# The second and third load on SyncE's queue, swapped, in a LayerNorm + S5 + SwiGLU kernel

## The chip, the cores and the metric

The kernel runs on one core of a Trainium2 chip. The metric is the device time of one execution in microseconds (us); lower is better. A profile is one execution seen by the hardware profiler, and its times count from the start of the span. TensorE (PE, with PEld for its weight loads), VectorE (DVE), ScalarE (ACT), GpSimd (POOL) and SyncE (SP) are the engines of the core. SyncE does no arithmetic here; it issues DMAs. ScalarE issues some as well, on a queue of its own.

## What is computed

The input x has 2048 rows of 512 in bfloat16. With xn the layer-normalised x, the result is the sum of x, a diagonal state-space model (S5) of xn and a SwiGLU block of xn:

```
xn  = layernorm(x)
Bu  = xn @ B_bar^T                 # complex, 512 states
h_t = Lam_bar * h_(t-1) + Bu_t     # over the 2048 rows
y   = 2 * real(h @ C^T) + xn * Dskip
ffn = (silu(xn @ w_gate) * (xn @ w_up)) @ w_down     # 1376 hidden columns
out = x + y + ffn
```

## The kernel before

The 2048 rows are 16 x tiles of 128 rows (`xall[:, n, :]`), and four tiles make a chunk of 512 rows. For a chunk, TensorE needs xnT, the transposed normalised rows, as its moving operand. The products with w_gate and w_up (`gu_mm`, L425; `w_last` L451 and L461), with B (`bproj_tile`, L350), with w_down (L505) and with C (L514) run over the chunks in an order that is written out by hand at the end of the kernel. VectorE's work (scan, rotations, tables, products) is put between them by a backlog with a cost for each operation, which `pump` works off.

w_gate and w_up are loaded in column groups (`fgroups`): group 0 holds the hidden columns of tiles 0 and 1, group 1 those of tiles 2 and 3, then 4 to 6 and 7 to 9. A group is one tile in SBUF, wg0 to wg3 for gate and wu0 to wu3 for up, and one DMA by `load_w1` (L110 to L112; all of them show as L112). Groups 0 and 1 have 256 KB each, in rows of 512 bytes. An x tile has 128 KB, in rows of 1024 bytes.

The loads are issued in program order on each engine (L123 to L154). Before the change SyncE issues x tile 0, wg0, x tile 2, wg1, wu1, x tiles 4 and 5, x tiles 6 and 7, wg2, wu2, the transposes of B's real part, wg3, wu3, and so on. ScalarE issues x tile 1 (held back behind a VectorE memset of a part of that tile, L124), wu0 and x tile 3. GpSimd loads three small parameter rows. Each DMA counts up one of eight completion semaphores, which the DMAs take in turn; a DMA that takes one for the second time is issued only when the earlier DMA on it has landed.

The first chunk is done tile by tile (the head, L600 to L650), because its tiles arrive one after the other:

- TensorE first runs nine warming matmuls that nobody reads (`dummy`, L574).
- For tile n, VectorE takes the row statistics (`ln_stats`, L178 and L179; L604 and L606 for tile 1, L619 and L621 for tile 3), ScalarE makes the inverse deviation (L183, L184), VectorE normalises (`norm_dve`, L196), TensorE transposes (`xT_pe`, L213), and VectorE (L220) or ScalarE (L222) copies the result from PSUM into xnT.
- Between these, `head_mm` (L597) multiplies the tiles that are there with the groups that are there: first tile 0 with wg0, then (after tile 1's transposes) tile 0 with wu0, tile 1 with both, then tiles 0 and 1 with hidden tile 2, which is the first use of wg1, then tile 2's transposes and the transpose of the parameter rows (L243), then wu1, and so on.

The engines wait only through semaphores, so a weight load that waits for its DMA holds up all TensorE instructions behind it.

Of the kernel before, what the change touches and what calls it, by code (L numbers as in the profile page):

```python
# [23 lines left out]
def kernel(  # L24
# [17 lines left out]
    nc = tc.nc  # L42
# [36 lines left out]
    x_v = A_x[0].rearrange("(n p) d -> p n d", p=128)  # L79
    out_v = out[0].rearrange("(n p) d -> p n d", p=128)  # L80
    wg_v = B_w_gate.rearrange("(k p) f -> p k f", p=128)
    wu_v = B_w_up.rearrange("(k p) f -> p k f", p=128)


    xall = const.tile([128, NT, D], BF16, name="xall")
# [3 lines left out]
    wg_g, wu_g = [], []  # L89
# [20 lines left out]
    def load_w1(q, tiles, view, gi):  # L110
        a, b = fgroups[gi]
        q.dma_start(out=tiles[gi][:], in_=view[:, :, a * 128:min(F, b * 128)])  # L112
# [10 lines left out]
    nc.sync.dma_start(out=xall[:, 0, :], in_=x_v[:, 0, :])  # L123
    nc.vector.memset(xall[:, 1, 0:D // 2], 0.0)  # L124
    nc.scalar.dma_start(out=xall[:, 1, :], in_=x_v[:, 1, :])
    load_w1(nc.sync, wg_g, wg_v, 0)
    load_w1(nc.scalar, wu_g, wu_v, 0)
    nc.sync.dma_start(out=xall[:, 2, :], in_=x_v[:, 2, :])
    nc.scalar.dma_start(out=xall[:, 3, :], in_=x_v[:, 3, :])
    load_w1(nc.sync, wg_g, wg_v, 1)  # L130
    load_w1(nc.sync, wu_g, wu_v, 1)
# [638 lines left out]
```

## Time and profile before

| what | value |
|---|---|
| time, median of 3 runs (lowest, highest) | 179.78 us (179.71, 179.78) |
| time of the profiled execution | 179.83 us |
| its span | 178.1 us |
| mean granted TensorE clock | 0.999 |
| TensorE, busy time | 173.7 us |
| VectorE, busy time | 153.3 us |
| DMA traffic over the whole span | 15.53 MB, mean 87 GB/s |
| SyncE's DMA queue (q1), ScalarE's (q10), share of 16 engines' time | 28.9%, 1.4% |

Busy time is the time in which an engine executes instructions; waits for semaphores are not in it. The chain of work that ended last is followed back from the last instruction, at each step to what released it. In the lists of instructions a line gives start and length in us, the engine (SPq and ACTq are DMA issues by SyncE and ScalarE), the line in the kernel, the operation, what it writes and reads, its shape and how many are merged; in brackets stands the idle time of the engine before it and what ended that idle time. "us to landing" of a DMA counts from the start of its issue to the last of its 16 completion counts.

### The profile page before, as it was taken

How to read it: one execution, taken by the hardware profiler on the slowest of the kernel's cores; microseconds unless marked ns; L12 is line 12 of the kernel's file. 1: busy time of each engine (PE TensorE's matmuls, PEld its weight loads, DVE VectorE, ACT ScalarE, POOL GpSimd, SP SyncE). 2: the span in 40 equal slices, each digit the busy share in tenths (PEclk: the TensorE clock that was granted, in tenths of full speed). 3: DMA queues.
4: the chain of work that ended last, by engine and by line, in shares of the span. 5: the costliest groups of instructions: out<-in, count | busy, mean ns of one | idle time of the engine just before them, and what ended most of it. 6: DMA issues, size and time to landing. Idle time of an engine off the chain costs nothing.

```text
span 178.1 us, 2462 instructions
## 1 busy us (share of the span) xinstructions
PE 173.7 (98%) x916; PEld 83.2 (47%) x916; DVE 153.3 (86%) x233; ACT 94.2 (53%) x173; POOL 23.2 (13%) x29
## 2 busy tenths in 40 slices
PE   7899999999999999999999999999999999999993
PEld 2784444444444444444444444444444444444743
DVE  3789997999999999999999999999999999940033
ACT  3579696978499966033997660024866610220000
POOL 6003000001400000029100000013405000150000
PEclk9999999999999999999999999999999999999999
DMA  5998956994236400021920000007286900073012
GB/s 159 327 254 204 144 98 174 361 184 104 44 76 218 180 0 0 0 29 14 137 61 0 0 0 0 4 0 81 29 125 84 156 2 0 0 79 39 4 48 70
DMA packets 29131, 15.53 MB, mean 87 GB/s; under 512 B 17824, under 2 KB 29056, under 8 KB 29088
## 3 DMA queue, kind: packets, MB, share of 16 engines
q1 hardware_dynamic: 24416, 11.41, 28.9%
q0 software_dynamic: 3456, 3.28, 14.5%
q10 hardware_dynamic: 1248, 0.69, 1.4%
q8 instruction: 7, 0.11, 0.3%
q14 instruction: 4, 0.03, 0.1%
HBM read 8.03 MB, written 5.24 MB: 75 GB/s over the span
## 4 chain that ended last, share of the span: by engine, by line
PE 96%; DMA 1%; DVE 1%; issue 0%
PE ps L425 36%; PE ps L505 21%; PE ps L514 16%; PE ps L350 16%; PE ps L597 3%; PE ps L451 2%; DMA xall<-in_A_x_dram 1%; PE ps L461 1%; PE ps L213 1%; DVE stats L178 0%; DVE stats L604 0%; DVE xall L196 0%; DVE res L517 0%; PE ps L574 0%; DVE mv L179 0%
## 5 line engine op out<-in xcount | busy, mean ns | idle before, releaser
L505 PE MATMUL ps<-wd_sb,guT 128*128 128x512 bf16 (+3 forms) x198 | 38.8, 355 | 0.0
L425 PE MATMUL ps<-xnT,wg 128*128 128x512 bf16 x148 | 38.0, 379 | 0.0
L425 PE MATMUL ps<-xnT,wu 128*128 128x512 bf16 x148 | 38.0, 379 | 0.0
L392 DVE TENSOR_TENSOR_SCAN g<-r_t,car,u 128x512 bf16<-128x512 f32 x24 | 28.9, 1265 | 0.0
L514 PE MATMUL ps<-CF,wt 128*128 128x512 bf16 (+2 forms) x144 | 28.3, 355 | 0.0
L350 PE MATMUL ps<-xnT,BT 128*128 128x512 bf16 x128 | 28.3, 379 | 0.0
L505 PEld LDWEIGHTS <-guT 128*128 128x128 bf16 (+1 forms) x198 | 18.5, 98 | 19.9
L521 ACT CAST res<-ps 128x512 bf16<-128x512 f32 x12 | 7.0, 585 | 38.5 <-PE ps L514 38.5
L439 ACT ACTIVATE guT<-ps 128x512 bf16<-128x512 f32 x40 | 24.8, 619 | 3.9 <-PE ps L425 3.7
L440 ACT CAST u<-ps 128x512 bf16<-128x512 f32 x40 | 24.2, 604 | 4.2 <-PE ps L425 4.2
L425 PEld LDWEIGHTS <-wu 128*128 128x128 bf16 x148 | 14.5, 98 | 17.5
L425 PEld LDWEIGHTS <-wg 128*128 128x128 bf16 x148 | 14.3, 98 | 17.6 <-issue 0.8
L522 POOL DMA_DIRECT2D out_dram<-res x12 | 11.1, 997 | 87.2 <-ACT res L521 87.2
L514 PEld LDWEIGHTS <-wt 128*128 128x128 bf16 x144 | 13.4, 98 | 14.3
L350 PEld LDWEIGHTS <-BT 128*128 128x128 bf16 x128 | 12.5, 98 | 15.1
L352 ACT CAST u<-ps 128x512 bf16<-128x512 f32 x32 | 17.5, 589 | 3.1 <-PE ps L350 3.1
L517 DVE TENSOR_TENSOR res<-ps,xn_end 128x512 bf16<-128x512 f32 (+2 forms) x6 | 3.0, 514 | 14.6 <-PE ps L514 14.6
L444 DVE TENSOR_TENSOR guT<-guT,u 128x1024 bf16<-128x1024 bf16 x20 | 13.5, 680 | 0.0
L178 DVE BATCH_NORM_STATS2 stats<-xall 128x6 f32<-128x512 bf16 x14 | 9.4, 670 | 1.9 <-DMA xall<-in_A_x_dram 1.9
L360 DVE TENSOR_TENSOR pm<-u,c 128x2048 bf16<-128x2048 bf16 x8 | 9.8, 1220 | 1.2 <-ACT c L277 1.1
L188 POOL TENSOR_TENSOR rstd<-ve,neg_half 128x4 f32<-128x4 f32 x3 | 5.3, 1750 | 40.7 <-DVE ve L187 40.7
L360 DVE TENSOR_TENSOR pm<-g,c 128x2048 bf16<-128x2048 bf16 x8 | 9.7, 1218 | 0.1
(103 smaller groups left out, 156.9 us busy)
## 6 DMA issues: line engine op xcount, KB each, us to landing
out_dram<-in_A_x_dram SPq DMA_DIRECT2D x1, 1536.0 KB, 8.0
out_dram<-res POOLq DMA_DIRECT2D x12, 128.0 KB, 3.2
out_dram<-xall POOLq DMA_DIRECT2D x3, 512.0 KB, 5.9
wd_sb<-in_B_w_down_dram SPq DMA_DIRECT2D x1, 1280.0 KB, 10.6
xall<-in_A_x_dram SPq DMA_DIRECT2D x1, 1024.0 KB, 5.9
wg<-in_B_w_gate_dram SPq DMA_DIRECT2D x2, 384.0 KB, 5.4
wu<-in_B_w_up_dram SPq DMA_DIRECT2D x2, 384.0 KB, 6.0
wg<-in_B_w_gate_dram SPq DMA_DIRECT2D x2, 256.0 KB, 4.5
```

Source lines behind the costliest of these rows:

```text
L178: nc.vector.bn_stats(out=stats[:, n, :], in_=xall[:, n, :])
L350: nc.tensor.matmul(ps[:], lhsT=BT[:, part, k, q * 128:(q + 1) * 128], rhs=xnT[:, k, c * CW:(c + 1) * CW], start=(k == 0), stop=(k == KD - 1))
L352: nc.scalar.copy(out=u_tiles[c][:, part, q, :], in_=ps[:])
L360: V.tensor_tensor(out=t[:], in0=flat(src()[:, i]), in1=flat(tab[:]), op=ALU.mult)
L392: V.tensor_tensor_scan(out=g()[:, part, q, :], data0=r_t[:, q:q + 1].to_broadcast([128, CW]), data1=u_tiles[c][:, part, q, :], initial=ini ...
L425: nc.tensor.matmul(ps[:fs, lo:hi], lhsT=wslice(groups, fi, k), rhs=xnT[:, k, c * CW + lo:c * CW + hi], start=(k == 0), stop=(k == KD - 1))
L439: nc.scalar.activation(out=guT[:fs, fi, :], in_=psg[:fs], func=ACT.Silu)
L440: nc.scalar.copy(out=u_pair[c][:fs, fi % 2, :], in_=psu[:fs])
L444: products.append(lambda: V.tensor_tensor(out=g, in0=g, in1=u, op=ALU.mult))
L505: nc.tensor.matmul(o[:], lhsT=gu_tiles[c][:fsz[fi], fi, i * 128:(i + 1) * 128], rhs=wd_sb[:fsz[fi], fi, lo:hi], start=(fi == 0), stop=False)
L514: nc.tensor.matmul(o[:], lhsT=w_tiles[c][:, part, q, i * 128:(i + 1) * 128], rhs=CF[:, part, q, lo:hi], start=False, stop=(part == 1 and q ...
L522: nc.gpsimd.dma_start(out=out_v[:, n, lo:hi], in_=res[:, lo:hi], accum_op=ALU.add)
```

## The change

x tile 2 is issued by SyncE directly behind x tile 0, and gate group 0 behind it. In the text of the kernel ScalarE's load of wu0 now stands ahead of SyncE's load of wg0; the order of ScalarE's own issues is as before. All loads have the sizes, sources and targets that they had. As x tile 2 now takes the second of the eight completion semaphores, wg0 the third and x tile 1 the fourth (they took the fourth, the second and the third), other later loads wait for them when the semaphores come round again.

```diff
     nc.sync.dma_start(out=xall[:, 0, :], in_=x_v[:, 0, :])
     nc.vector.memset(xall[:, 1, 0:D // 2], 0.0)
     nc.scalar.dma_start(out=xall[:, 1, :], in_=x_v[:, 1, :])
+    nc.sync.dma_start(out=xall[:, 2, :], in_=x_v[:, 2, :])
+    load_w1(nc.scalar, wu_g, wu_v, 0)
     load_w1(nc.sync, wg_g, wg_v, 0)
-    load_w1(nc.scalar, wu_g, wu_v, 0)
-    nc.sync.dma_start(out=xall[:, 2, :], in_=x_v[:, 2, :])
     nc.scalar.dma_start(out=xall[:, 3, :], in_=x_v[:, 3, :])
     load_w1(nc.sync, wg_g, wg_v, 1)
     load_w1(nc.sync, wu_g, wu_v, 1)
```

## The prediction

> **What bounds the kernel now.** I read the page's busy shares first, then the chain of work that ended last, then the instructions of the first 10 us in order of time, and last the landings of the DMAs issued there.
>
> ```profile
> PE 173.7 (98%) x916; PEld 83.2 (47%) x916; DVE 153.3 (86%) x233; ACT 94.2 (53%) x173; POOL 23.2 (13%) x29
> ...
> PE 96%; DMA 1%; DVE 1%; issue 0%
> ```
>
> TensorE is busy for 173.7 of 178.1 us, and 96% of the chain is TensorE. So there is no slack behind the head: the chain in order of time shows where TensorE still waits.
>
> ```profile
> 4.96 0.40 PE ps L213 x4
> 5.36 0.23 PE ps L574 x4
> 5.59 0.04 issue
> 5.63 0.62 PE ps L597 x8
> 6.25 0.22 PE ps L213 x4
> 6.47 1.40 PE ps L597 x24
> 7.88 0.01 issue
> 7.89 0.61 PE ps L597 x4
> ```
>
> From 5.63 to the last matmul at 175.24 TensorE only follows itself. What delays it in the head delays the end one for one, unless a later wait of the head swallows it. So the instructions of the head matter (start, length, idle time before and its releaser):
>
> ```profile
> 1.19 0.42 SPq L112 DMA_DIRECT2D wg<-in_B_w_gate_dram  x1
> ...
> 1.65 0.50 SPq L128 DMA_DIRECT2D xall<-in_A_x_dram  x1
> ...
> 5.28 0.29 DVE L220 COPY xnT<-ps 128x256 bf16<-128x256 bf16 x1 [0.29 <-PE ps L213]
> ...
> 5.37 0.10 PEld L597 LDWEIGHTS <-wg 128*128 128x128 bf16 x1
> ...
> 5.92 0.69 DVE L178 BATCH_NORM_STATS2 stats<-xall 128x6 f32<-128x512 bf16 x1
> ...
> 7.88 0.33 PEld L597 LDWEIGHTS <-wg 128*128 128x128 bf16 x4 [0.18 <-DMA wg<-in_B_w_gate_dram]
> ```
>
> The two swapped loads are the SyncE issues at 1.19 and 1.65. Gate group 0 (wg0) is first read by the weight load at 5.37; its matmul at 5.63 waits not for it but for the xnT copy that VectorE ends at 5.57. x tile 2 is first read at 5.92. And at 7.88 a weight load waits 0.18 us for gate group 1 (wg1). The landings (issue to landing, of the DMAs in flight at 1.6 to 1.7 us):
>
> ```profile
> wg<-in_B_w_gate_dram SPq DMA_DIRECT2D x1, 256.0 KB, 3.4
> wu<-in_B_w_up_dram ACTq DMA_DIRECT2D x1, 256.0 KB, 4.3
> xall<-in_A_x_dram SPq DMA_DIRECT2D x1, 128.0 KB, 4.1
> ```
>
> Added to the issue times 1.19, 1.55 and 1.65, and read to two digits from the landing events: wg0 lands at 4.55, up group 0 (wu0) at 5.85, x tile 2 at 5.79. In the same way x tile 1 lands at 3.64, x tile 3 at 6.79, wg1 at 7.84, up group 1 (wu1) at 8.74.
>
> **The change, part by part.**
>
> Removed and added: nothing. TensorE, VectorE, ScalarE and GpSimd keep their instructions in the same order; SyncE keeps its instructions and swaps two of them. ScalarE's own loads (x tile 1, wu0, x tile 3) keep their order.
>
> x tile 2 earlier: worth 0. It lands at 5.79, but VectorE is busy up to 6.00 (the normalisation of tile 1, 5.59 + 0.41) before it reads it. The tile has had 0.2 us to spare; landing earlier leaves that VectorE instruction where it is.
>
> wg0 later: this is the cost. Its issue moves from 1.19 to about 1.65. In its queue it then has x tile 2 ahead, and ScalarE's wu0 (issued 1.55) is no longer behind but ahead of it or beside it. Bounds for its landing t: early, the old 4.55 plus the later issue, 0.46: 5.0. Late within the same work: by 5.85 the old kernel had landed the same five transfers (x tiles 0 to 2, wg0, wu0; x tile 3 partly too), and the DMA share is 0.92 to 1.11 in every stretch from 2.6 to 9.0 us, so the order decides who is last but not when all are done. The last of wg0 and wu0 therefore lands near 5.85, and I expect it to be wg0 or both. I take t = 5.75, nearest to the row of x tile 2 (5.79), which held the same place on the queue: issued at 1.65, behind all those bytes.
>
> How the two queues share the DMA engines speaks to that. From 3.2 to 3.6 us the view of the queues gives SyncE's (q1) everything, though ScalarE's wu0 had been issued 1.6 us before:
>
> ```profile
> q1 hardware_dynamic: 243, 0.12, 106.9%
> q10 hardware_dynamic: 2, 0.00, 0.9%
> ```
>
> The Trainium skill, "DMA: Bandwidth & Descriptors", section "Queues, rings and completion order", has each engine alternate between queues packet by packet; by that rule wg0 and wu0 would end together, at about 5.85 for this kernel, and the sum below would be +0.13. The row of 3.2 to 3.6 shows no alternation, that of 4.0 to 5.0 does (68.4% for q10, 38.0% for q1), so both stay possible.
>
> From t to TensorE: wg1's weight load started at 7.884, 0.04 after its landing, and the second matmul behind it at 8.007, 0.12 later, since the first weights could not be loaded ahead. So the second matmul of the wg0 block starts at t + 0.04 + 0.12 = t + 0.17, where it now starts at 5.683: a delay of d = t - 5.52 (if positive). At t = 5.75, d = 0.23. Behind the waiting weight load stand the eight matmuls of L597, the four transposes of x tile 1, and through them ScalarE's two xnT copies at 6.40 and the statistics of tile 2. All of these shift by d.
>
> What swallows it: 0.02 at 5.869 (a matmul that waited for ScalarE's copy), then the wait for wg1. Without it the block of 7.88 would have started at 7.715; its second matmul stands at 8.007 in place of 7.824, so 0.18 is swallowed there. The SyncE issues of wg1 and wu1 keep their times and the bytes ahead of them are the same, so their landings should stay. The next candidate, the weight load for wu1 at 8.779, starts 0.04 after that landing, but it also follows a 12-column transpose after which the array changes shape: the same gap stands before that transpose (8.502 to 8.650), where no load was late. So no slack is counted there. The sum: loss = max(0, d - 0.20) = max(0, t - 5.72). At 5.75 it is +0.03; at t = 5.0, nothing; at 5.85, +0.13.
>
> VectorE's side keeps up: the shifted copies move the normalisation of tile 2 from 7.51-7.92 to 8.15 at d = 0.23, and its transposes load at 8.23. That cover ends at d = 0.27, later than TensorE's own 0.20, and then costs no more than TensorE's own delay.
>
> x tile 1 now shares the engines from about 2.25 with x tile 2 in place of wg0. It lands at 3.64 and is read at 3.81 when VectorE comes free: 0.17 of cover. Gone, it would move the first normalisation and the first matmul; bounds are 0 and the 0.37 us that a 128 KB tile takes of 16 engines (128 packets at 46 ns / 16) less 0.17, 0.20, again swallowed by wg1's wait. I count 0.
>
> Waits that move on SyncE: eight completion semaphores are used in turn, and x tile 2, wg0 and x tile 1 have changed places on them. The load of x tiles 6 and 7, issued at 4.57, waited for wg0 (4.55); now for x tile 2, so it goes some 0.5 earlier. Up group 2 waited for x tile 2, now for x tile 1, long landed. But gate group 2, issued at 4.98, waited for x tile 1 and now waits for wg0: it goes at t + 0.02. Behind it stand its own issue (0.47), that of up group 2 (0.50 to 0.87, rows of SyncE) and then the eight transposes of B, with gaps of 0.05: the first goes at t + 1.09 to t + 1.46 in place of 6.72, at t = 5.75 0.1 to 0.5 later. Their cover: B's last block lands at 22.30, and its first reader, the twentieth matmul of L350, is due at 19.04 + 19 x 0.216 = 23.15, 0.85 later. Gate group 2 landed at 11.43, 1.2 after the load ahead of it on its queue, and is read at 13.65. At t = 5.75 all of this costs nothing; from t = 6.1 the transposes use up their 0.85 and TensorE would wait once more.
>
> Total: 179.83 us of the profiled execution (span 178.1 and 1.7 around it) + 0.03 = 179.86. The median of the runs shown is 0.05 below it, 179.78, which would give 179.81. I give 179.85.
>
> **The rivals.**
>
> *Slower: x tile 3 passes wg0.* If wu0, issued 0.1 us before wg0, is served first, then x tile 3, next on ScalarE's queue, is free early and takes its turns ahead of wg0's end. For it: wu0's queue had 68.4% of 4.0 to 5.0. Against it: x tile 3 is issued 0.4 after wg0. Price: t between 5.85 + 0.37 (one tile's share) = 6.22 and x tile 3's own old landing, 6.79; at 6.25 the loss is 0.53: 180.4, in which the 0.15 that the transposes of B would be late is already contained. It decides from t = 6.08, where the loss passes 0.36. Chance 0.25.
>
> *Slower: a later landing moves.* Either B's last block comes over 0.85 late although wg0 does not, since the eight transposes lie closer to other loads than before (as much again late, 0.5, gives 180.3), or wg1 and wu1 do: if the order at the front leaves the engines empty for a moment, every later landing moves and no wait swallows it: 0.4 us late gives 180.2. Against it are the slack of 0.85 and the full DMA share. Chance 0.07.
>
> *Slower: the TensorE clock.* The nine warming matmuls up to 4.27 stood 0.43 us apart, at half the later pace (0.216 for 512 columns); after 0.69 us of idleness the next came at full pace. If the wait for wg0 brought the half pace back for as long again (3.49 us), it would cost 1.75: 181.6. The Trainium skill, "TensorE: Matmul & The Clock Gate", section "What's actually happening", asks for a whole idle window of about 3.4 us for that; the idle 0.69 here agrees. Chance 0.03.
>
> *Faster.* wg1 lands earlier because DMA engines fill better at the start with two 1 KB-row tiles. All there is to win is the 0.18 at 7.88: 179.65, and this stays within 0.2%. Beyond 0.2% the head shows nothing to win; chance 0.06 for what I don't see.
>
> *No effect at all:* wg0 lands before 5.55, wu0 last: 179.8, which can't be told from the forecast.
>
> **How the numbers follow.** 0.2% is 0.36 us, about what a measurement of this kernel can tell from no change. The forecast (t between 5.0 and 6.08, loss 0 to 0.36, the no-effect and the small-gain case with it) has 0.59. Slower is 0.25 + 0.07 + 0.03 = 0.35, faster 0.06. The range reaches from 179.6 (the whole of wg1's wait won) to 180.4 (x tile 3 passing at 6.25): it leaves out the larger half of the slow cases and the unseen gain, some 0.2.
>
> **What would show it.** Right: x tile 2 lands near 4, wg0 between 5.5 and 5.9, the first L597 matmul at 5.8 to 5.9 with wg0 as releaser, no wait for wg1 left at 7.88, and everything behind it in its old place. Wrong: wg0 past 6.1, or wg1 and wu1 off their 7.84 and 8.74, or matmuls of the head at double spacing.

## The result and the profile after

The changed kernel takes 180.66 us (median of 20 runs, 179.89 to 182.23), the kernel before 179.78 us (median of 20 runs beside them, 179.45 to 180.20). The ratio is 1.0058, with a 95% interval from 1.0041 to 1.0075: the change costs about 0.9 to 1.0 us. The forecast was 179.85, with a range of 179.6 to 180.4; the time lies above it.

The profiled execution took 179.89 us, which happens to be the fastest of the 20. It shows what the prediction expected. First the instructions of the head (start, length, idle time before and its releaser):

```profile
1.19 0.42 SPq L126 DMA_DIRECT2D xall<-in_A_x_dram  x1
1.65 0.99 SPq L112 DMA_DIRECT2D wg<-in_B_w_gate_dram  x2
...
5.30 0.29 DVE L220 COPY xnT<-ps 128x256 bf16<-128x256 bf16 x1 [0.40 <-PE ps L213]
...
5.91 0.45 PEld L597 LDWEIGHTS <-wg 128*128 128x128 bf16 x8 [0.34 <-DMA wg<-in_B_w_gate_dram]
5.92 0.62 PE L597 MATMUL ps<-xnT,wg 128*128 128x128 bf16 x8 [0.16 <-DVE xall L196]
...
7.95 0.37 PEld L597 LDWEIGHTS <-wg 128*128 128x128 bf16 x4
```

The weight load for wg0, which went at 5.37 before, now waits until 5.91 for the DMA, though the half of xnT that its matmul reads is there at 5.59. The matmul behind it carries another releaser, the normalisation of tile 1 that ended at about the same moment; it can't be the cause, since before the same matmul ran at 5.63 with that normalisation ending at 6.00. At 7.95 no wait for wg1 is left: it has been swallowed. In the chain everything behind keeps its spacing and ends 0.08 later than before:

```profile
5.93 0.61 PE ps L597 x8
6.54 0.22 PE ps L213 x4
6.76 1.84 PE ps L597 x28
...
175.32 0.02 issue
175.34 0.29 DVE res L517
```

So this execution can't tell where 0.9 us went. A second profile of the same kernel, taken in the first experiment, can.

### The profile page after: what moved, and what is told of

It is laid out like the page before. It is cut to its first block, busy times and chain, and to the rows that moved or that the text cites. A ratio compares the mean times of both kernels' runs of the same rounds, so it can differ in the third digit from the quotient of the medians.

```text
span 178.1 us, 2462 instructions
## 1 busy us (share of the span) xinstructions
PE 174.3 (98%) x916; PEld 83.4 (47%) x916; DVE 153.1 (86%) x233; ACT 94.3 (53%) x173; POOL 23.2 (13%) x29
## 3 DMA queue, kind: packets, MB, share of 16 engines
HBM read 8.03 MB, written 5.24 MB: 75 GB/s over the span
## 4 chain that ended last, share of the span: by engine, by line
PE 95%; DVE 2%; DMA 1%; ACT 0%; issue 0%
PE ps L425 36%; PE ps L505 21%; PE ps L514 16%; PE ps L350 16%; PE ps L597 3%; PE ps L451 2%; DMA xall<-in_A_x_dram 1%; PE ps L461 1%; DVE xall L196 0%; DVE stats L178 0%; PE ps L213 0%; DVE stats L604 0%; ACT ve L183 0%; DVE res L517 0%; ACT rstd L184 0%
```

## The experiments

"Landing" is the last of a DMA's 16 completion counts, and its *median* the mean of the eighth and ninth count; both are read from the landing events of the trace. A *lag* is the last count less the median. "After" is the profile shown above; e1, e2 and so on are the profiles of the runs whose labels (e1_again, e2_fill, ...) begin so.

**1. The changed kernel once more (e1_again).** No edit.

> The changed kernel once more, for a second profiled execution and a second set of times. Theory C (the TensorE clock): the wait for gate group 0 lies in the stretch in which TensorE is still warming up, and in most executions it makes the half pace last longer; so times are spread over 1 us or more (about 179.9 to 182.2), gate group 0 lands near 5.9 in every profile, and in a slower execution the matmuls behind 5.9 us still start 0.107 us apart for 128 columns. Theory L (the landing): gate group 0 lands at a different time in each execution, near 6.6 in a typical one and near 8 in the slowest; the matmuls behind it then start 0.055 apart. Theory B (B's transposes): the head looks as in the first profile and TensorE waits near 23 us.

Measured: 180.79 us (7 runs, 180.02 to 181.57), ratio 1.0054 (1.0034 to 1.0074). Its profiled execution took 181.01 us, and its head differs from the one above (instructions from 5 us on):

```profile
6.99 0.37 SPq L112 DMA_DIRECT2D wg<-in_B_w_gate_dram  x1
7.02 0.45 PEld L597 LDWEIGHTS <-wg 128*128 128x128 bf16 x8 [1.63 <-DMA wg<-in_B_w_gate_dram]
7.02 0.62 PE L597 MATMUL ps<-xnT,wg 128*128 128x128 bf16 x8 [1.46 <-DMA wg<-in_B_w_gate_dram]
```

The chain of this execution names the DMA, from its issue to its landing, and behind it the same TensorE pieces as before, only later:

```profile
1.65 5.32 DMA wg<-in_B_w_gate_dram
6.97 0.05 issue
7.02 0.62 PE ps L597 x8
7.64 0.22 PE ps L213 x4
7.87 1.84 PE ps L597 x28
...
13.48 6.91 PE ps L425 x32
20.39 6.91 PE ps L350 x32
```

The pieces have their old lengths (1.84 for the 28 matmuls), so TensorE runs at full pace; and the products with B from 20.39 on wait for nothing. Issue to landing of the DMAs in flight at 1.6 to 1.7 us, the first profile of the changed kernel and then this one:

```profile
wu<-in_B_w_up_dram ACTq DMA_DIRECT2D x1, 256.0 KB, 4.0
wg<-in_B_w_gate_dram SPq DMA_DIRECT2D x1, 256.0 KB, 4.2
xall<-in_A_x_dram SPq DMA_DIRECT2D x1, 128.0 KB, 2.7
```

```profile
wu<-in_B_w_up_dram ACTq DMA_DIRECT2D x1, 256.0 KB, 5.0
wg<-in_B_w_gate_dram SPq DMA_DIRECT2D x1, 256.0 KB, 5.3
xall<-in_A_x_dram SPq DMA_DIRECT2D x1, 128.0 KB, 2.7
```

Same kernel, same queues, same x tile 2 (2.7 us): but wg0 needs 4.2 us in one execution and 5.3 in the other. The counts say how: the median count of wg0 stands at 5.64 in the first and at 5.72 in the second, the last at 5.87 and at 6.97. In the second 13 of the 16 counts were in by 6.15, and the last two came at 6.67 and 6.97. By this trace the theory "the landing varies" holds.

**2. TensorE kept busier in the wait (e2_fill)**: in the changed kernel, `dummy(4, 128)` (L609) becomes `dummy(9, 128)`.

> The changed kernel with nine in place of four warming matmuls of 128 columns behind the first transposes, so that TensorE has less idle time while it waits for gate group 0. Theory C: the half pace ends earlier in most executions; the median comes down from 180.66 towards 179.9 to 180.2. Theory L: the matmuls only fill a wait; the median stays within 0.1 of the changed kernel's, or is higher. Theory B: no change.

Measured: 180.41 us, ratio 1.0034 (1.0020 to 1.0048); its profile took 180.74 us with wg0 landing at 6.69. The nine matmuls end at 6.33, and a wait of 0.40 us for wg0 is left behind them. The median lies between what the two theories named (179.9 to 180.2, or within 0.1 of 180.66), and its interval overlaps with that of experiment 1. So filling most of the wait does not bring the time back; whether it wins a small part isn't shown.

**3. The same idleness without a late load (e3_idle)**: in the kernel before, VectorE gets 0.69 us of statistics that nobody reads, so that the first wg0 matmul goes at 5.93.

```diff
     rstd_act(1)
+    lag = const.tile([128, 6], F32, name="lag")
+    nc.vector.bn_stats(out=lag[:], in_=xall[:, 0, :])
     xT_pe(0, on_dve=(0,))
```

> The kernel before, with its old order of loads and one more row statistics of x tile 0 on VectorE ahead of the first xnT copy, whose result nobody reads: the first matmuls then start about 0.38 later, at 6.0, with no DMA moved. Theory C: the times spread as those of the changed kernel do, median 180.3 to 180.8, and the half pace lasts past 6 us in a slower execution. Theory L and theory B: only the shift counts, 0.38 less the 0.2 swallowed by the wait for gate group 1 and at most 0.1 more by VectorE's own delay: 179.9 to 180.1, spread as before.

Measured: 179.81 us, ratio 1.0004 (0.9995 to 1.0012). The first matmul stands where the first profile of the changed kernel has it (5.92), 0.30 later than before:

```profile
5.93 0.74 PE L597 MATMUL ps<-xnT,wg 128*128 128x128 bf16 x8
```

0.30 less the 0.20 that the prediction counts as swallowed is +0.10; the profile took 179.97 us, 0.14 more than that of before, and the interval holds 0.10 too. The block takes 0.74 us here in place of 0.62, because its first matmuls still run at half pace (0.107 us apart); in this execution the half pace of the start ends at 6.2. A TensorE that starts 0.30 late costs no more than the formula says, and the times show none of the changed kernel's spread (179.67 to 180.10). A longer idleness without a late load was not tried.

**4 and 5. The other load first (e4_up_first, e5_before_up_first)**: the head multiplies tile 0 with wu0 first and with wg0 after tile 1's transposes; once in the changed kernel, once in the kernel before.

```diff
-    head_mm(0, 0, 1, range(0, HK), (0, 1))
-    head_mm(0, 0, 1, range(HK, KD), (0, 1))
+    head_mm(1, 0, 1, range(0, HK), (0, 1))
+    head_mm(1, 0, 1, range(HK, KD), (0, 1))
     xT_pe(1)
     rstd_act(2)
-    head_mm(1, 0, 1, range(0, HK), (0, 1))
-    head_mm(1, 0, 1, range(HK, KD), (0, 1))
+    head_mm(0, 0, 1, range(0, HK), (0, 1))
+    head_mm(0, 0, 1, range(HK, KD), (0, 1))
```

> The changed kernel with tile 0 multiplied by up group 0 first, and by gate group 0 only behind the transposes of tile 1. Up group 0 landed at 5.54 in the profile of the changed kernel, so the first matmul should start at 5.6 and gate group 0 is needed at 6.3 only. Theory C: the idle time is nearly that of before, so the median goes back to 179.7 to 179.9. Theory L: gate group 0 at a typical 6.6 still holds TensorE up by 0.3, and the median falls by about 0.6 at most, to 180.0 to 180.2. Theory B: no change, 180.6.

> The kernel before, its loads untouched, with tile 0 multiplied by up group 0 first and by gate group 0 behind tile 1's transposes. Up group 0 lands at 5.85 to 5.9 there, later than its new first use at 5.63. Theory 'order' (the swap itself makes single DMA engines fall behind, by up to 1 us, since both groups 0 now start together behind the x tiles): with the old order no engine falls far behind, the first matmul starts at 5.9 to 6.1, and the median is 179.8 to 180.0 with the narrow spread of before. Theory 'cover' (engines fall behind as much in the old order, and gate group 0's 1.1 us of spare time hid it): the median is 180.3 to 180.8 with a spread of over 1 us.

Measured: 180.12 us for the changed kernel so, ratio 1.0011 (1.0000 to 1.0022): most of the loss is gone when wg0, which landed at 6.24 here, is first needed at 6.78. The profile still shows a wait of 0.37 us, now for wu0 (6.01). And 180.29 us for the old order so, ratio 1.0034 (1.0021 to 1.0048): there wu0 is the load that is waited for. Its profile gives, for the loads in flight at 1.6 to 1.7 us and the weight load that waits:

```profile
wg<-in_B_w_gate_dram SPq DMA_DIRECT2D x1, 256.0 KB, 3.1
wu<-in_B_w_up_dram ACTq DMA_DIRECT2D x1, 256.0 KB, 4.8
xall<-in_A_x_dram SPq DMA_DIRECT2D x1, 128.0 KB, 4.2
```

```profile
6.35 0.45 PEld L597 LDWEIGHTS <-wu 128*128 128x128 bf16 x8 [1.01 <-DMA wu<-in_B_w_up_dram]
```

In the old order too a load of the second rank lands late (wu0 here at 6.31, in the kernel before at 5.85); there it was only not yet needed. wg0 landed early, at 4.25. The old order has the lag as well (wu0's is 0.93 here), but under cover.

**6. wu0 moved to SyncE's queue, behind wg0 (e7_one_queue)** (changed kernel; ScalarE keeps x tiles 1 and 3).

> The changed kernel with up group 0 taken off ScalarE's queue and put behind gate group 0 on SyncE's (x tiles 0 and 2, gate 0, up 0, gate 1, up 1; ScalarE loads x tiles 1 and 3). Theory 'side by side' (the two groups 0 of 512-byte rows, served at once from two queues, delay each other and leave single engines behind): gate group 0 lands by 5.2 and the first matmul starts at 5.6; up group 0, now last, lands near 5.9 to 6.3; median 179.7 to 180.1. Theory 'behind x tile 2' (its later place on SyncE's queue alone makes gate group 0 late): it still lands at 5.9 or later in most executions, and the median stays at 180.4 to 180.9.

Measured: 180.75 us, ratio 1.0051 (1.0034 to 1.0069). wg0's median count came to 4.93, earlier by 0.7, but its last to 6.09, and wu0 landed at 7.30; TensorE waits for both. 0.47 of the loss is no matter of the head, as experiment 11 tells: from the end of TensorE's last matmul to the start of the kernel's last instruction it took 3.25 us in place of 2.78.

**7. x tile 2 ahead of wu0, not of wg0 (e8_x2_on_act)**: the kernel before, with x tile 2 on ScalarE's queue between x tile 1 and wu0.

> The kernel before with x tile 2 moved from SyncE's queue to ScalarE's, ahead of up group 0 (SyncE: x tile 0, gate 0, gate 1, up 1; ScalarE: x tiles 1 and 2, up 0, x tile 3). x tile 2 is early as in the change, but gate group 0 keeps its place. Theory 'displaced gate group': gate group 0 lands at 4.6 to 5.0, up group 0 at 5.9 to 6.3 beside its use at 6.26, gate group 1 a little earlier than 7.84; median 179.6 to 180.0. Theory 'early x tile' (any load of 1 KB rows put second disturbs the start of the queues): spread and median like the changed kernel's, 180.4 to 180.8.

Measured: 181.45 us, ratio 1.0119 (1.0082 to 1.0156), in two groups: four runs at 181.06 to 181.48, and two at 183.07 and 183.14 with a mean clock of 0.991. The profile is of the slowest, 183.14. wg0 lands at 4.51 as in the old order; wu0's median is 6.72 and its last count 8.03, and TensorE waits for it. Here the load that gave up its place is the late one.

**8 and 9. Without the three parameter rows (e9_after_no_prm, e10_before_no_prm)**: GpSimd's loads are left out and the rows filled with a constant, so other parameters are computed; once in the changed kernel, once in the kernel before.

```diff
-    for i, v in enumerate((A_Lambda_re, A_Lambda_im, A_log_dt)):
-        nc.gpsimd.dma_start(out=prm_rows[...], in_=...)
+    nc.gpsimd.memset(prm_rows[:], -0.5)
```

> The changed kernel without GpSimd's three loads of parameter rows; the rows are set to -0.5 on the chip, so the state-space part computes with other parameters. Theory 'parameter rows' (these 256-byte transfers, which appear in the trace from 3.2 us on, are what makes single DMA engines fall behind): with them gone the 16 counts of gate group 0 come within 0.5 us, it lands at 5.6 to 5.9 in every execution, and the median falls from 180.7 to 179.8 to 180.0 with a spread under 0.8. Theory 'own traffic' (engines fall behind on the large loads themselves): gate group 0's last count still comes 0.4 to 1.5 us behind its median, and the median stays at 180.4 to 180.9.

> The kernel before without the same three loads, rows set to -0.5. Theory 'parameter rows': gate group 1 and up group 1 lose their late last count (7.84 and 8.74 against 7.18 and 8.02 for the count before), TensorE's wait at 7.88 goes, and the median falls by 0.1 to 0.2, to 179.5 to 179.65. Theory 'own traffic': 179.7 to 179.85 as before.

Measured: 180.92 us, ratio 1.0099 (1.0063 to 1.0135), and 179.63 us, ratio 1.0001 (0.9991 to 1.0011). The lag stays (wg0 in the changed kernel: median 5.67, last 6.44): these small loads aren't needed for it. The 179.63 lies where the theory 'parameter rows' put it, but the kernel before took 179.65 beside it, so nothing was won.

**10. wg0 late, with x tile 2 behind it (e11_gate_late)**: the kernel before, with a VectorE memset of wg0 that holds its issue back to 1.63. x tile 2 follows at 2.08.

```diff
+    nc.vector.memset(wg_g[0][:], 0.0)
     nc.scalar.dma_start(...)                # x tile 1
     load_w1(nc.sync, wg_g, wg_v, 0)
```

> The kernel before, its order of loads kept, with gate group 0's issue held back until VectorE has cleared its tile, to about 1.65 us; x tile 2 and all later loads of SyncE come some 0.45 later as well. Theory 'bytes ahead' (what makes gate group 0 late in the change is x tile 2 and up group 0 ahead of it): it lands at 4.7 to 5.2, its first matmul stays at 5.63, and the loss is only what x tile 2, now near 6.2, and the groups 1 cost: 179.8 to 180.2. Theory 'late slot' (a load issued at 1.65 is served together with up group 0 and falls into the time in which engines fall behind): it lands at 5.4 to 6.5, and the median is 180.3 to 181.

Measured: 181.32 us, ratio 1.0098 (1.0060 to 1.0135). This median stands between two groups, four runs at 180.42 to 180.55 and four at 182.10 to 182.84; the profile, 182.56, is of the second. Nothing but x tile 0 is ahead of wg0 on its queue, and still it lands at 6.96 (median 6.18): being issued just behind wu0 (1.51) is enough in this execution, x tile 2 need not be ahead. This profile shows one thing more (stretch, length, busy time of PE, PEld, DVE, ACT, POOL, then granted clock, DMA share, GB/s):

```profile
6.00:7.00 1.00, 0.00 (x0) 0.00 (x1) 0.00 (x0) 0.00 (x0) 0.00 (x0) 1.00 1.12 350
7.00:8.00 1.00, 1.00 (x15) 1.00 (x16) 0.52 (x1) 0.21 (x1) 0.00 (x0) 0.80 1.18 315
8.00:9.00 1.00, 1.00 (x12) 1.00 (x11) 0.94 (x4) 0.92 (x4) 0.00 (x0) 0.50 1.14 324
11.00:12.00 1.00, 1.00 (x12) 0.82 (x11) 0.59 (x3) 0.00 (x0) 0.00 (x0) 1.00 1.28 318
```

TensorE did nothing from 5.5 to 7.0 us. Soon after that its granted clock is 0.50, until 11 us, when it is full again. With the 0.80 from 7 to 8 that makes about 3.4 us at half pace, by my estimate up to 1.7 us of delay; the mean clock of this execution is 0.991. In experiment 1 TensorE waited as long, from 5.56 to 7.02, and kept full pace.

In the changed kernel 17 of the 20 runs took 179.89 to 181.27 us and three 182.04 to 182.23. All 20 have a mean clock of 0.998 or more, which rules out a second stretch at half pace like this one. It doesn't rule out that the half pace of the start lasted longer, since the column of the granted clock doesn't show that stretch: in the first profile of the changed kernel it stands at 1.00 from 4 to 5 us, though the four transposes of tile 0 take 0.61 us there, in place of 0.40 in the kernel before:

```profile
4.87 0.61 PE L213 MATMUL ps<-ident,xall 128*128 128x128 bf16 x4
```

So why these three were dear is open; no profile shows one. The median doesn't hang on them: without them it is 180.64 in place of 180.66.

**A run that told little (e12_up_behind_x3)**: the changed kernel with ScalarE's order x tile 1, x tile 3, wu0.

> The changed kernel with up group 0 behind x tile 3 on ScalarE's queue, so that SyncE issues gate group 0 (1.65) ahead of up group 0 (about 2.0). Theory 'up group 0 ahead' (what makes gate group 0 late is above all the other group's earlier issue): most of gate group 0's 16 counts come near 4.9, its last one by 5.5, the first matmul is at 5.63 to 5.7, and up group 0, needed at 6.3, becomes the late one with a landing near 6.3 to 6.8; median 180.0 to 180.4. Theory 'place behind x tile 2': most counts still come at 5.3 or later, the last at 5.9 to 7, and the median stays at 180.5 to 181.

Measured: 180.49 us, ratio 1.0052 (1.0030 to 1.0073); wg0's median is 5.18, its last count 6.33. The median count came 0.5 earlier, and a lag of 1.15 ate it.

**11. All loads of the head but x tile 1 on SyncE's queue (e13_all_on_sync, e14_old_one_queue)**, first in the new order (x0, x2, wg0, wu0, x3, wg1, wu1), then in the old (x0, wg0, x2, wu0, x3, wg1, wu1).

> All early loads but x tile 1 on SyncE's queue, in the order x tiles 0 and 2, gate 0, up 0, x tile 3, gate 1, up 1. Theory 'two queues' (single DMA engines fall behind because two queues take turns on them): the 16 counts of every load come within 0.6 us, gate group 0 lands by 5.3 and up group 0 by 6.2; median 179.7 to 180.2. Theory 'any order' (single engines fall behind from about 4 us on, whatever the queues): gate group 0's last count comes 0.7 to 1.5 behind its median, at 5.6 to 6.5, up group 0 near 7, and the median is 180.4 to 181.2.

> Old order of x tile 2 and gate group 0, with all loads but x tile 1 on SyncE's queue (x0, wg0, x2, wu0, x3, wg1, wu1). Theory 'two queues': single DMA engines fall behind because two queues feed them at once; then the last counts of wg0 and wu0 both lie within 0.3 us of the count before them, the time equals that of the kernel before (179.8 us, ratio 0.999 to 1.001) or is better by the 0.18 us wait for gate group 1. Rival 'any loaded engine': the lag comes with the load on the engines whatever the queue; then wg0 still lands by 4.7 (nothing but x0 and x1 ahead of it), but up group 0, x tile 3 or gate group 1, which are now later in one row, show last counts 0.3 to 1 us behind their median and the ratio lies at 1.001 to 1.005.

Measured: 180.40 us, ratio 1.0030 (1.0017 to 1.0042), and 180.21 us, ratio 1.0021 (1.0011 to 1.0031). The traces (179.99, the fastest of its nine runs, and 180.09) contradict these times if one thinks of the head: TensorE's last matmul ends at 174.96 and at 175.06, ahead of the 175.23 of the kernel before. In them the loss is behind it. From there to the start of the last instruction it took 3.21 us in both; in the kernel before and in every trace with as many SyncE instructions as there (82) it was 2.70 to 2.79. The longer part begins behind the wait for the last store. So both got back the DMA counts of the kernel before, 50 on SyncE and 6 on ScalarE (e15_old_one_queue_tail, e16_new_one_queue_tail): two stores of the end (around 171 and 172.5 us) go to ScalarE. Their two waits leave SyncE with them, so its instructions are 80 and not, as the first text below says, as many as before.

```diff
-                    (nc.sync if b == D else nc.scalar).dma_start(...)
+                    (nc.sync if b == D and n > NT - 3 else nc.scalar).dma_start(...)
```

> Old order with all loads but x tile 1 on SyncE, and in exchange two of the stores at the end (around 171 and 172.5 us) on ScalarE, so that each engine has as many instructions as in the kernel before. Theory 'the rest was the ending': with two DMAs more on SyncE, the ending behind the last store took 0.44 us longer (3.22 us from TensorE's last matmul to the last instruction, 2.78 in the kernel before) while TensorE ended 0.17 earlier; with the counts as before, the ending is 2.75 to 2.8 again and the ratio 0.998 to 1.000. Rival: the lagging loads cost the time in typical executions; then the ratio stays at 1.001 to 1.003 whatever the ending does.

> New order (x0, x2, wg0) with all loads but x tile 1 on SyncE, and the same two stores on ScalarE. Theory 'two queues': alone on one queue, gate group 0 lands by about 5.0, 0.7 before TensorE would wait, in nearly every execution; without the longer ending the ratio is 0.998 to 1.001, so that the same swap of x tile 2 and gate group 0 costs nothing here. Rival 'any loaded engine': gate group 0 still lands past 5.7 in typical executions, ratio 1.002 to 1.005.

Measured: old order 179.75 us, ratio 0.9997 (0.9987 to 1.0006); new order 179.87 us, ratio 1.0004 (0.9992 to 1.0015). The ending is 2.71 us in both. **On one queue the same swap of x tile 2 and wg0 shows no loss against the kernel before.** The medians of the two are 0.12 apart, and the upper end of the second interval leaves room for 0.27 us. The head of the new order so:

```profile
5.75 0.45 PEld L597 LDWEIGHTS <-wg 128*128 128x128 bf16 x8 [0.40 <-DMA wg<-in_B_w_gate_dram]
...
6.82 0.45 PEld L597 LDWEIGHTS <-wu 128*128 128x128 bf16 x8 [0.39 <-DMA wu<-in_B_w_up_dram]
```

That was an unlucky execution (180.06 us): wg0's median stood at 4.57, its last count at 5.71, a lag of 1.14 us. By the prediction's formula wg0 costs nothing up to 5.72; what this execution lost (the last matmul ends at 175.56, 0.33 later than before) came behind that, with the wait for wu0, which landed at 6.78. And it settles a second point: lags of a microsecond come on one queue as well (in the old order on one queue wu0 had its median at 5.38 and its last count at 6.67). The theory that two queues at once make single engines lag, which the profile of e14_old_one_queue had seemed to support (wg0's lag 0.13, wu0's 0.41), falls.

None of these versions beats both kernels: the best, the old order on one queue, equals the kernel before.

## Why the prediction was wrong

The landings of wg0 in all traces sort the cases (us; loss begins at 5.72):

| order of the loads | median count | last count | lag |
|---|---|---|---|
| old, two queues (before, e3, e5, e10) | 4.17 to 4.36 | 4.25 to 4.63 | 0.08 to 0.37 |
| old, one queue (e14, e15) | 4.08, 4.08 | 4.21, 4.79 | 0.13, 0.71 |
| new, one queue (e13, e16) | 4.53, 4.57 | 4.99, 5.71 | 0.46, 1.14 |
| new, two queues (after, e1, e2, e4, e9) | 5.64 to 5.80 | 5.87 to 6.97 | 0.23 to 1.25 |
| new, wu0 on SyncE behind wg0, x tile 3 on ScalarE (e7) | 4.93 | 6.09 | 1.16 |
| new, x tile 3 ahead of wu0 on ScalarE (e12) | 5.18 | 6.33 | 1.15 |
| x tile 2 on ScalarE, wg0 second on SyncE (e8) | 4.16 | 4.51 | 0.34 |
| old, wg0 issued at 1.63 (e11) | 6.18 | 6.96 | 0.77 |

**The step that failed** is the bound of t: "late within the same work: by 5.85", with the ground that "the order decides who is last but not when all are done", and t = 5.75 from it. The 5.85 was the landing of wu0 in one execution. As a bound for the median count it is good: 5.64 to 5.80 were measured, around the 5.75 chosen. But a weight load waits for the last of 16 counts, and this lies 0.23 to 1.25 us behind the median, differently in each execution. The Trainium skill, "DMA: Bandwidth & Descriptors", section "Why a DMA increments its semaphore by 16 and not by 1", says that the engines of a DMA finish independently and that only the full 16 means landed; the trace agrees (13 counts by 6.15, the last at 6.97), and the prediction counted only bytes and a mean share. In the old order the lag was there too, but wg0's median lay 1.4 to 1.6 us ahead of the point where loss begins, more than any lag of it seen. The swap used up this spare time, which no wait in the profile of before shows.

**The formula held.** loss = t - 5.72, on 179.83:

| profile | wg0 lands | by the formula | measured |
|---|---|---|---|
| after | 5.87 | 179.98 | 179.89 |
| e9 | 6.44 | 180.55 | 180.49 |
| e2 | 6.69 | 180.80 | 180.74 |
| e1 | 6.97 | 181.08 | 181.01 |

All four lie 0.06 to 0.09 below the formula, most of it because the second matmul of the block starts 0.11 behind the landing (5.98 in the first profile, 7.09 in experiment 1), where the prediction took 0.17 from a block of 256 columns. The middle of these four landings, 6.57, gives a loss of 0.85; the medians differ by 180.66 - 179.78 = 0.88. With four executions of kernels that differ a little, so close a match is partly luck. The mechanism was right and the term was mis-sized: 0.03 against 0.88.

Point by point:

- *The bound, the path, what is swallowed*: right. TensorE's chain behind the head keeps its spacing, and most of a small delay is swallowed: in the first profile wg0's block is 0.35 late by d = t - 5.52 (0.30 by its second matmul), the end 0.08.
- *x tile 2 earlier is worth nothing*: right; it lands at 3.83 to 3.96, its reader starts when VectorE is free.
- *Where wg0's time goes*: not to its place behind x tile 2. On one queue this place moves the median from 4.08 to 4.53 and 4.57, and no loss shows. The rest, 1.1 to 1.3 us up to the 5.64 to 5.80 of two queues, is the work beside it: on two queues wg0 shares the DMA engines with wu0, which it had behind it before. The rule of the Trainium skill that the prediction weighed ("DMA: Bandwidth & Descriptors", section "Queues, rings and completion order": queues alternate packet by packet) has wg0 and wu0 end together, and the traces agree: in the four profiles of the new order that read wg0 first they land within 0.20 to 0.43 of each other. The time by it, +0.13, rests on the same 5.85 and has the same fault.
- *x tile 3 passes wg0* (the rival whose size fits best, 180.4): wrong as a mechanism; in experiment 1 x tile 3 lands at 7.20, behind wg0. Its t of 6.22 to 6.79 was the right region for another reason.
- *The waits of SyncE*: gate group 2 did wait for wg0 (issued at 5.89 and at 6.99 in place of 4.98). That TensorE would wait once more from t = 6.1 was wrong: in experiment 1, with t = 6.97, the first transpose of B goes at 7.96 in place of 6.72, but B's last block lands at 21.73, ahead of the 22.30 of the kernel before, and its reader, 1.19 later than before like all of TensorE, is due at 24.33. A later first transpose did not make the last landing later.
- *The clock*: not in the median. But the ground given against it was too strong. The Trainium skill, "TensorE: Matmul & The Clock Gate", section "What's actually happening", asks for a whole idle window of about 3.4 us; in experiment 10 half pace came after 1.5 us of idleness, in experiment 1 it did not. The measurement decides: 1.5 us can be enough, and need not be. The rows of the warming matmuls were misread too: the last two of the nine start only 0.38 and 0.22 us after the ones before them, so in the profile of before the half pace ended at about 3.6 us, ahead of the idle 0.69. In other profiles it lasts longer, to 6.2 in e3.
- *A small misreading*: the DMA share is 1.12 from 7.0 to 8.0 us, above the 1.11 given as the highest; nothing rests on it.
- *The chances*: 0.25 for the rival with this size was for a special mechanism. What was missing was a case "a load lands later in most executions than in the one shown".

**Open**: why the last counts of a load fall behind by up to 1.4 us in some executions (wg0 by up to 1.25, wg1 in e8 by 1.39). Neither the parameter rows (experiments 8 and 9) nor a second queue of loads (11) is needed for it. Whether the place of the data in DRAM matters was not tried. Why the ending takes 0.45 us more with one or two more SyncE DMAs is not explained either; shown is only that it goes when the DMA counts are as before. The count alone is not a rule: in e8, with one DMA less on SyncE and one more on ScalarE, the ending took 2.95.

## What to carry to other kernels

The spare time of a load is to be held against the spread of its landings, not against the one landing of a profile: look at the 16 counts, and profile twice before calling a microsecond of spare time free. In this kernel the load that the first matmul waits for did best near its queue's front with no other large load beside it; when it stood second, its neighbours did less harm on the same queue behind it. And when a variant moves instructions between engines, compare TensorE's last matmul as well as the time, so that a longer ending isn't taken for a slower head.

## What the hardware showed

- One and the same 256 KB load, issued at the same moment (1.65), landed at 5.87 in one execution and at 6.97 in another, with medians only 0.08 apart.
- With one or two DMAs moved to SyncE the ending of the kernel was 0.43 to 0.47 us longer (3.21 to 3.25 us against 2.78).
- Half clock for about 3.4 us after 1.5 us of idle TensorE (granted clock 0.80 from 7 to 8 us, 0.50 from 8 to 11 us, 1.00 from 11 us on), in some executions only.
